# Which products of a six-group MoE kernel run in two Winograd levels: the third factor made one stage earlier, P7 of the third group split again

## The chip, the cores and the metric

The kernel runs on one core of one Trainium2 chip. Its metric is the device time of one execution in microseconds (us), lower is better; a run's time is given as the median of several executions. The profile is of one further execution, with every instruction's start and length on the core's engines: TensorE (PE, with its weight loads as PEld), VectorE (DVE), ScalarE (ACT), GpSimd (POOL) and SyncE (SP). GpSimd does no arithmetic here: it issues the software DMAs, one after the other. SyncE issues the hardware ones.

## The reference

A block of linear attention with decay, whose output is the input of a two-layer block with the activation h − tanh(h). All is in float32.

```python
# q, k, v: (B 4, H 8, S 768, D 64), blocks of 64 along S, lam one decay per head
intra = einsum('bhic,bhjc->bhij', qb, kb) * Dmask      # Dmask = lam ** (i - j), i >= j
out   = einsum('bhij,bhjd->bhid', intra, vb) + einsum('bhid,bhde->bhie', qb * lam_pow, kv_state)
kv_state = lam ** 64 * kv_state + einsum('bhsd,bhse->bhde', kb * rev_pow, vb)
# x: attention's output as (B*S 3072, H*D 512)
h = x @ w_in              # w_in  512 x 2048
g = h - tanh(h)
y = g @ w_out             # w_out 2048 x 512
```

## The kernel before, in words

**Groups and stages.** The 768 positions are cut into six groups of 128 (`g` from 0 to 5, `NG` 6), each with the 512 tokens of four batches. A group has an *up stage* (x @ w_in and the activation), a *down stage* (g @ w_out), and, in pieces laid between the products, the attention of the group after it. The loop over `g` from 1 on is one Python loop that writes the order out by hand. What is called the second group here is `g` = 1, the third `g` = 2 (the constant `GI`).

**Products.** The large matrix products are done by Winograd's form of Strassen's scheme: each matrix is cut in four, and seven products of sums of the quarters, P1 to P7, take the place of eight. `FACT` names the two sums that each product takes. In the down stage the right-hand sums come from w_out alone. They are made once, while the first group is in its down stage, and lie in DRAM in the tensor `factors`.

**Two levels.** A product can be split once more, into seven products of sums of quarters of its two factors. `twice(g, n)` says whether product n of the down stage of group g is done so. The plain form is `down`: four weight pieces of 256 KB and 16 matmuls of 256 columns, which the trace records as 32. The form in two levels is `down_twice`: seven pieces of 256 KB and 28 matmuls of 128 columns, recorded as 56. Ahead of it, `sums_twice` makes three sums of the left factor on VectorE; inside it, ScalarE copies four results out of PSUM and VectorE makes one more sum of the left factor and adds the rest up. In the kernel before, P5 and P6 are in two levels in the second group; P4, P5 and P6 in the third; all of P3 to P7 in the fourth and fifth; all but P3 in the sixth.

**Making a factor's second level.** The right-hand sums of the second level have to be made on the chip too. `MADE` gives the order of the factors: P5's, P6's, P4's, P7's, P3's, with the index t from 0 to 4. Each takes three steps. `load_quarters(t)` loads the factor's four quarters from `factors` (four DMAs of 256 KB, L770). `quarters_alone(t)` copies three quarters, that serve as they are, to the DRAM tensor `fine` (three DMAs, L775). `factors_twice(t)` makes four differences on VectorE (L782), in place in the quarters' buffers, and stores each to `fine` (four DMAs, L783). Since the differences are made in place, they must wait until `quarters_alone` has read the buffers.

In the kernel before, t = 0 and 1 are loaded ahead of the second group's up stage, and `make_factors(step)` runs their differences inside it, one difference after each of certain products: `TURNS` gives the steps, 7 to 10 and 14 to 17 of 28. A step is one product P1 to P7 of one of the four slices u of the up stage. t = 2 is loaded in the second group's down stage and its differences made in the tail of that stage; t = 3 and t = 4 likewise in the third group's, each in a buffer that a sum of the up stage (`hidden(..., "S1")`) leaves free.

**Pieces.** `piece` loads weight pieces for the down stage in the order of a list, `stream`, up to eight ahead (`RING`), into the eight buffers of the tag "wb". The quarters of t = 0 lie in the same eight buffers, those of t = 1 in buffers of output tiles.

**Other work in the second group's up stage.** `inner_weights` makes sums of w_in on VectorE (L651) for the third group and stores them (L654); `up` does the products and the activation: L576 and L581 add a PSUM bank called z to a sum, L564 subtracts the tanh; L332 and L343 belong to the next group's attention. SyncE loads q and k of later groups in small blocks.

**What sets the order.** Each engine runs its instructions in one order. A planning pass of the framework sets it: by place in the program, but an instruction that it takes to be ready sooner can be put ahead of earlier ones. `keep_in_program_order` (through `tied`) pins an instruction behind the one traced just before it on its engine. The differences in `factors_twice` are pinned on VectorE, the loads for t > 1 on GpSimd; the copies in `quarters_alone`, the stores and the piece loads are not.

Of the kernel before, what the change touches and what calls it, by code (L numbers as in the profile page):

```python
# [24 lines left out]
def kernel(  # L25
# [39 lines left out]
    NG = S // BLK  # L65
# [61 lines left out]
    def tied(yes, op):  # L127
        return tc.keep_in_program_order(op) if yes else op
# [68 lines left out]
    GI = 2  # L197
    TWICE = (3, 5, 6, 4, 7)
# [96 lines left out]
    def bank(name, tag, bufs):  # L295
        return psum.tile([128, 512], F32, name=name, tag=tag, bufs=bufs)
# [242 lines left out]
    def hidden(g, c):  # L539

        if (g, c) not in hid:
            hid[g, c] = gpool.tile([128, NU, 2, HB], F32, name=f"g{c}", tag=f"g{c}")
        return hid[g, c]
# [179 lines left out]
    RING = 8  # L723

    def twice(g, n):
        return n in TWICE and not (g == NG - 1 and n == 3) and not (g == 1 and n == 4) and not (
            g <= GI and n in (7, 3))

    def in_turn(g):

# [8 lines left out]
    def pieces_of(g):  # L739
        for n in (1, 2, 4, 5, 6, 7):  # L740
            yield from ((g, n, x) for x in (SUB if twice(g, n) else range(NU)))
        if g == NG - 1:
            yield from ((g, 3, x) for x in range(NU))
            return
        for kind, x in in_turn(g):
            if kind == "down":
                yield g, 3, x
            elif x in (3, 5, 6):
                yield g + 1, ("in", kind), x
# [7 lines left out]
    def quarter_source(t, i, j):  # L757
        return factors[XAT[FACT[MADE[t]][1]]].rearrange("p (u m) c -> p u m c", m=2)[:, :, i, ts(j, 128)]

    def load_quarters(t):  # L760

        for i in range(2):
            for j in range(2):
                if t == 0:
                    x = late["pool"].tile([128, NU, 128], F32, name="wq", tag="wb", bufs=RING)
                elif t > 1:
                    x = hidden(GI + (t > 2), "S1")[:, 2 * i + j].rearrange("p m (v c) -> p (m v) c", v=2)
                else:
                    x = opool.tile([128, NU, 128], F32, name="oq", tag="o")
                tied(t > 1, nc.gpsimd.dma_start(out=x, in_=quarter_source(t, i, j)))  # L770
                quarters[t, i, j] = x

    def quarters_alone(t):
        for x, i, j in ((1, 0, 0), (2, 1, 0), (3, 1, 1)):
            nc.gpsimd.dma_start(out=fine[TWICE.index(MADE[t]), SUB.index(x)], in_=quarters[t, i, j])  # L775

    def factors_twice(t):

        b11, b12, b21, b22 = (quarters.pop((t, i, j)) for i in range(2) for j in range(2))
        t1, t3, t4, t2 = b11, b12, b21, b22  # L780
        for x, dst, a, b in ((5, t1, b12, b11), (7, t3, b22, b12), (6, t2, b22, t1), (4, t4, b21, t2)):
            tc.keep_in_program_order(nc.vector.tensor_tensor(dst, a, b, op=AL.subtract))  # L782
            nc.gpsimd.dma_start(out=fine[TWICE.index(MADE[t]), SUB.index(x)], in_=dst)  # L783
            yield
# [21 lines left out]
    def stores_due():  # L806
        while due:
            due.pop(0)(True)

    def store(g, c, t, late_store=False):  # L810
        i, j = divmod(c - 11, 10)
        rows = out.rearrange("(b s) d -> s b d", b=B)[ts(g, BLK), 2 * i:2 * i + 2, ts(j, 256)]
        eng = nc.sync if g == NG - 1 else nc.gpsimd

        def go(held):
            tied(held, eng.dma_start(out=rows, in_=t.rearrange("q (m c) -> q m c", m=2)))

        if late_store:
            due.append(go)
        else:  # L820
            go(False)

    def otile(name):
        return opool.tile([128, 512], F32, name=name, tag="o")

    res, low = {}, {}
# [56 lines left out]
    def quarter(g, n):  # L883

        a = hidden(g, HIDAT[FACT[n][0]])
        return tuple(a[:, :, j, ts(i, 128)] for i in range(2) for j in range(2))
# [9 lines left out]
    def down_twice(g, n, zw):  # L896
        a11, a12, a21, a22 = quarter(g, n)
        s1, s2 = low.pop((g, n))
        y = bank("y2", "ya" if n in (4, 6, 3) else "yb", 1)[:, 0:128]
        zw = bank("zw", zw, 1)  # L900
        o = res[g, n] = otile(f"q{n}")
        for x, a, dst, keep in ((1, a11, y, o[:, 0:128]), (2, a12, zw[:, 0:128], None), (6, s2, y, o[:, 128:256]),
                                (5, s1, zw[:, 256:384], None), (7, a21, y, o[:, 384:512]), (3, a12, zw[:, 128:256], None),
                                (4, a22, y, o[:, 256:384])):
            wb = piece(g, n, x).rearrange("p m c -> p (m c)")
            for u in range(NU):
                tied(held["yes"], nc.tensor.matmul(  # L907
                    out=dst, lhsT=a[:, u, :], rhs=wb[:, ts(u, 128)], start=x in (1, 2) and u == 0, stop=u == NU - 1,
                    skip_group_check=True))
            if keep is not None:  # L910
                nc.scalar.activation(keep, dst, AF.Copy)  # L911
            if x == 2:
                nc.vector.tensor_tensor(a12, a12, s2, op=AL.subtract)
            if x == 5 and due:
                stores_due()
            if x != STEPS[-1]:
                yield

        o5 = o.rearrange("q (i c) -> q i c", i=2)[:, :, 128:256]
        nc.vector.tensor_tensor(o5, o5, zw[:, 256:384][:, None, :].to_broadcast([128, 2, 128]), op=AL.add)  # L920
        nc.vector.tensor_tensor(o[:, 0:256], o[:, 0:256], zw[:, 0:256], op=AL.add)
        if n == 6:

            nc.vector.tensor_tensor(o, o, res[g, 1], op=AL.add)
            for x in (4, 5):
                nc.vector.tensor_tensor(res[g, x], res[g, x], o, op=AL.add)
        elif n == 7:
            nc.vector.tensor_tensor(res[g, 4], res[g, 4], o, op=AL.add)
            store(g, 21, res[g, 4], g < NG - 1)
            nc.vector.tensor_tensor(o, o, res[g, 5], op=AL.add)  # L930
            store(g, 22, o, g < NG - 1)
        elif n == 3:
            nc.vector.tensor_tensor(o, o, res[g, 5], op=AL.add)
            store(g, 12, o)
        yield

    def every(steps):
        for _ in steps:
            pass
# [82 lines left out]
    def run(pieces):  # L1022
        for fn, *args in pieces:
            fn(*args)
# [90 lines left out]
    late["pool"] = ctx.enter_context(tc.tile_pool(name="late", bufs=1))  # L1115


    TURNS = {t + x: n for n, t in ((0, 7), (1, 14)) for x in range(4)}
    making = {}

    def make_factors(step):
        t = TURNS.get(step)
        if t is not None:
            if t not in making:
                making[t] = factors_twice(t)
            next(making[t])

    for t in range(2):
        load_quarters(t)
# [4 lines left out]
    for g in range(1, NG):  # L1134
# [69 lines left out]
            for u in (2, 3):  # L1204
                inner_weights(u, (5,))
        if g < GI:
            load_quarters(2)
        if twice(g, 7):
            sums_twice(g, 7)
        every(down_twice(g, 6, zw[0]))  # L1210
# [3 lines left out]
        p7 = down_twice(g, 7, zw[1]) if twice(g, 7) else down(g, 7)  # L1214
        next(p7)
        run(p1[4:])
        if g == GI:
            load_quarters(3)
        if g < GI:
            for u in (0, 1):  # L1220
                inner_weights(u, (6,))
# [1 line left out]
        if last:  # L1223
            down_end(g)
            continue
        if g in (1, GI):
            quarters_alone(1 + g)
        if g < GI:
            for u in (2, 3):
                inner_weights(u, (6,))  # L1230
# [5 lines left out]
        for kind, x in in_turn(g):  # L1236
            if (kind, x) == (5, 1):
                inner_tokens(g + 1, (5, 2))
                every(parts[1])
                every(p3)  # L1240
            if (kind, x) == (4, 1):
                inner_tokens(g + 1, (4, 6))
                every(parts[5])
                every(parts[2])
                if g >= GI:
                    run(early_pieces)
            if kind not in parts:
                parts[kind] = inner_steps(g + 1, kind)
            next(parts[kind])
            if kind == 1 and x in ((6, 3) if g >= GI else (3,)):  # L1250
                run(early_pieces[:1])
                early_pieces = early_pieces[1:]
            if g < GI and (kind, x) == (4, 5):
                every(factors_twice(2))
            if g == GI and (kind, x) == (1, 4):
                every(factors_twice(3))
            if g == GI and (kind, x) == (5, 7):
                load_quarters(4)
            if g == GI and (kind, x) == (4, 2):
                quarters_alone(4)  # L1260
            if g == GI and (kind, x) == (6, 7):
                every(factors_twice(4))
            if kind == 6 and x in (5, 6, 2, 7):
                seeded(g + 1, (5, 6, 2, 7).index(x), 11)
                if g < GI and x == 6:
                    run(early_pieces)
# [32 lines left out]
```

## Time and profile before

| | |
|---|---|
| median of 3 runs | 645.86 us (643.43 to 646.31) |
| the profiled execution | 642.59 us, span 640.8 us |
| TensorE busy | 632.3 us, 99% of the span, granted clock 1.00 |
| VectorE, ScalarE, GpSimd busy | 480.7, 270.9, 221.6 us |
| data moved by DMA | 139.80 MB, mean 218 GB/s |
| second group: first up to last inner product | about 139 to 276 us |
| third group, from its first down matmul to that of the fourth | 275.80 to 376.99 us |

Times within the span count from its start. "L850" is line 850 of the kernel: L850 are the plain down products, L907 those in two levels, L554 the up products of the second group, L698 and L620 those of the later groups; L796 loads a piece of a factor in two levels, L799 a plain one. Matmul ends are modelled in the trace, so distances are read from start to start. A busy TensorE is not in itself one at its peak.

### The profile page before, as it was taken

The page shows a single profiled execution, that of the slowest core. Times are in us where ns is not written, and L with a number is a line of the kernel's source. Part 1 is how long each engine was busy: PE and PEld are TensorE (multiplying, and loading weights), DVE is VectorE, ACT ScalarE, POOL GpSimd, SP SyncE. Part 2 cuts the span into 40 slices and gives each one's busy share as a digit, 9 for nine tenths or more (in the row PEclk, how much of TensorE's full clock was granted, in tenths as well). Part 3 has the DMA queues.
Part 4 walks back from the last instruction along what each step waited for, and adds up shares of the span by engine and source line. Part 5 has one row for each costly group of instructions (what it writes and reads, how often), then busy time and mean ns, then how long its engine had stood idle before and what let it go on. Part 6 is the DMA issues. An engine that isn't in the chain of part 4 may idle for free.

```text
span 640.8 us, 16604 instructions
## 1 busy us (share of the span) xinstructions
PE 632.3 (99%) x6424; PEld 580.8 (91%) x6424; DVE 480.7 (75%) x956; ACT 270.9 (42%) x626; POOL 221.6 (35%) x388
## 2 busy tenths in 40 slices
PE   8999999999999999999999999999999999999998
PEld 6788888888888999998999998999998899998997
DVE  4779697757888877579966589987658987467953
ACT  3898678403522422335431336243246332334310
POOL 0000135436623465311545730445321254421251
PEclk9999999999999999999999999999999999999999
DMA  9989899749956899876899994898873477732384
GB/s 211 230 230 246 224 280 303 268 120 287 306 134 171 244 298 316 234 159 132 246 272 279 268 318 111 212 278 266 226 194 77 136 240 239 247 107 76 100 300 144
DMA packets 166046, 139.80 MB, mean 218 GB/s; under 512 B 136720, under 2 KB 137872, under 8 KB 165968
## 3 DMA queue, kind: packets, MB, share of 16 engines
q0 software_dynamic: 31648, 104.62, 50.4%
q1 hardware_dynamic: 134176, 34.12, 26.2%
q8 instruction: 51, 0.84, 0.5%
q14 instruction: 27, 0.22, 0.1%
q10 hardware_dynamic: 144, 0.00, 0.0%
HBM read 111.94 MB, written 26.74 MB: 216 GB/s over the span
## 4 chain that ended last, share of the span: by engine, by line
PE 79%; issue 10%; POOL 4%; DMA 3%; DVE 2%; SPq 1%; ACT 1%; POOLq 0%
PE plain L850 12%; PE y L698 8%; PE y L907 8%; PE acc L995 7%; PE y L554 7%; PE zw L907 6%; PE z L698 4%; PE y L620 3%; PE zs L620 3%; PE z L554 3%; PE h L966 3%; POOL wb L796 2%; PE w L698 2%; PE w L554 2%; PE op L498 2%
## 5 line engine op out<-in xcount | busy, mean ns | idle before, releaser
L796 POOL DMA_DIRECT2D wb<-fine x133 | 71.6, 539 | 156.8 <-PE plain L850 107.9
L850 PE MATMUL plain<-wb,g 128*128 128x256 f32 x416 | 96.0, 381 | 0.0
L850 PEld LDWEIGHTS plain<-wb,g 128*128 128x128 f32 x416 | 77.5, 190 | 10.4
L911 ACT ACTIVATE q<-y 128x128 f32<-128x128 f32 x76 | 21.1, 277 | 85.2 <-PE y L907 84.1
L799 POOL DMA_DIRECT2D wb<-factors x64 | 34.5, 539 | 62.4 <-PE z L698 40.4
L907 PE MATMUL y<-wb,g 128*128 128x128 f32 x336 | 44.8, 278 | 0.0
L793 POOL DMA_DIRECT2D wb<-fine_in x60 | 32.5, 543 | 27.8 <-PE z L698 10.8
L601 ACT ACTIVATE th<-g 128x512 f32<-128x512 f32 x48 | 29.5, 627 | 29.4 <-DVE g L626 29.3
L907 PEld LDWEIGHTS y<-wb,g 128*128 128x128 f32 x336 | 40.7, 192 | 0.7
L689 ACT ACTIVATE g<-y 128x512 f32<-128x512 f32 x24 | 14.3, 597 | 63.1 <-PE y L698 63.1
L218 POOL DMA_DIRECT2D raw<-in_moe_w_out_dram x12 | 7.1, 592 | 87.8 <-ACT r L290 84.1
L401 ACT ACTIVATE k_nat<-k_nat,mask 128x64 f32<-128x64 f32 (+1 forms) x128 | 35.0, 336 | 0.6 <-DMA k_nat<-in_k_dram 0.6
L995 PE MATMUL acc<-wt,g 128*128 128x256 f32 x144 | 32.7, 380 | 0.0
L602 DVE TENSOR_TENSOR g<-g,th 128x512 f32<-128x512 f32 x48 | 32.0, 683 | 0.4
L698 PE MATMUL z<-tt,wb 128*128 128x128 f32 x256 | 31.9, 275 | 0.0
L966 PE MATMUL h<-xt,w 128*128 128x256 f32 x128 | 29.9, 383 | 1.2 <-DVE w L293 1.2
L995 PEld LDWEIGHTS acc<-wt,g 128*128 128x128 f32 x144 | 27.0, 190 | 4.1 <-DVE g L1003 0.4
L620 PE MATMUL y<-xt,w 128*128 128x256 f32 x128 | 30.3, 379 | 0.0
L620 PE MATMUL zs<-xt,ws 128*128 128x256 f32 x128 | 30.2, 379 | 0.0
L698 PEld LDWEIGHTS z<-tt,wb 128*128 128x128 f32 x256 | 30.2, 192 | 0.0
L907 PE MATMUL zw<-wb,g 128*128 128x128 f32 x224 | 30.1, 277 | 0.0
L966 PEld LDWEIGHTS h<-xt,w 128*128 128x128 f32 x128 | 23.6, 190 | 4.6 <-ACT xt L459 0.8
(237 smaller groups left out, 1541.6 us busy)
## 6 DMA issues: line engine op xcount, KB each, us to landing
wb<-fine POOLq DMA_DIRECT2D x133, 256.0 KB, 4.1
wb<-factors POOLq DMA_DIRECT2D x64, 256.0 KB, 4.4
wb<-fine_in POOLq DMA_DIRECT2D x60, 256.0 KB, 4.6
v_nat<-in_v_dram SPq DMA_DIRECT2D x24, 256.0 KB, 5.0
raw<-in_moe_w_out_dram POOLq DMA_DIRECT2D x12, 512.0 KB, 5.6
fine<-gS POOLq DMA_DIRECT2D x21, 256.0 KB, 6.0
k_nat<-in_k_dram SPq DMA_DIRECT2D x20, 256.0 KB, 5.3
raw<-in_moe_w_in_dram SPq DMA_DIRECT2D x8, 512.0 KB, 5.1
```

The source lines that it names most:

```text
L401: tc.keep_in_program_order(nc.scalar.activation(k_h, k_h, AF.Copy, scale=mask[0:rows, h % 2, h // 2, HALF - 1:HALF]))
L554: tied(held["yes"], nc.tensor.matmul(out=t[:, m, :], lhsT=wt[:, kt, ts(m, 128)], rhs=x[:, kt, :], start=first and m == 0 and kt == 0, stop ...
L602: nc.vector.tensor_tensor(dst(c), src, th, op=AL.subtract)
L620: nc.tensor.matmul(out=t[:, m, :], lhsT=wt[:, kt, ts(m, 128)], rhs=x[:, kt, :], start=False, stop=kt == 1, skip_group_check=True)
L698: nc.tensor.matmul(out=dst[:, ts(u, 128)], lhsT=a, rhs=b, start=(x in (1, 5) or x == 2 and not filled) and u == 0, stop=True, skip_group_c ...
L793: nc.gpsimd.dma_start(out=t.rearrange("p m c -> p (m c)"), in_=fine_in[INNER.index(n_[1]), (5, 6, 3).index(x_)].rearrange("p u c -> p (u c)"))
L796: nc.gpsimd.dma_start(out=t.rearrange("p m c -> p (m c)"), in_=fine[TWICE.index(n_), SUB.index(x_)].rearrange("p u c -> p (u c)"))
L799: nc.gpsimd.dma_start(out=t, in_=factors[XAT[FACT[n_][1]]][:, 2 * x_:2 * x_ + 2, :])
L850: tied(held["yes"], nc.tensor.matmul(out=t[:, m, :], lhsT=a[:, u, kt, ts(m, 128)], rhs=wb[:, kt, :], start=first and u == 0 and m == 0 and ...
L907: tied(held["yes"], nc.tensor.matmul(out=dst, lhsT=a[:, u, :], rhs=wb[:, ts(u, 128)], start=x in (1, 2) and u == 0, stop=u == NU - 1, skip ...
L966: tied(u == 0 or held["yes"], nc.tensor.matmul(out=hm[c][:, m, :], lhsT=w1[u][:, i, a, ts(m, 128)], rhs=xt[0, t][:, i, :], start=m == 0 an ...
L995: tied(held["yes"], nc.tensor.matmul(out=acc[n][:, r, :], lhsT=a[:, ts(r, 128)], rhs=b, start=kt == 0 and r == 0, stop=kt == KH - 1, skip_ ...
```

## The change

P7 of the third group is done in two levels. For that, the second level of P7's factor (t = 3) has to be there by the third group, so it is made where P4's (t = 2) was, in the second group's down stage, in the same buffer; and t = 2 moves to the second group's up stage: its quarters are loaded at step 11 into four of the eight piece buffers, its three copies follow in the program after step 17, and its differences come after steps 18 to 21. The work for t = 3 goes from the third group's tail; t = 4 stays there. Whether P7's two output stores are put off is now asked by `twice(g, 3)` instead of `g < NG - 1`: for the third group they are issued at once, as its plain P7's were.

```diff
     def twice(g, n):
-        return n in TWICE and not (g == NG - 1 and n == 3) and not (g == 1 and n == 4) and not (
-            g <= GI and n in (7, 3))
+        return n in TWICE and not (g == NG - 1 and n == 3) and not (g < GI and n in (4, 7)) and not (
+            g <= GI and n == 3)
...
     def load_quarters(t):
-                if t == 0:
+                if t in (0, 2):
                     x = late["pool"].tile([128, NU, 128], F32, name="wq", tag="wb", bufs=RING)
                 elif t > 1:
-                    x = hidden(GI + (t > 2), "S1")[:, 2 * i + j].rearrange("p m (v c) -> p (m v) c", v=2)
+                    x = hidden(GI + (t > 3), "S1")[:, 2 * i + j].rearrange("p m (v c) -> p (m v) c", v=2)
...
         elif n == 7:
-            store(g, 21, res[g, 4], g < NG - 1)
+            store(g, 21, res[g, 4], twice(g, 3))
-            store(g, 22, o, g < NG - 1)
+            store(g, 22, o, twice(g, 3))
...
-    TURNS = {t + x: n for n, t in ((0, 7), (1, 14)) for x in range(4)}
+    TURNS = {t + x: n for n, t in ((0, 7), (1, 14), (2, 18)) for x in range(4)}
     def make_factors(step):
         t = TURNS.get(step)
         if t is not None:
             if t not in making:
                 making[t] = factors_twice(t)
             next(making[t])
+        if step == 11:
+            load_quarters(2)
+        if step == 17:
+            quarters_alone(2)
...
         if g < GI:
-            load_quarters(2)
+            load_quarters(3)
...
         next(p7)
         run(p1[4:])
-        if g == GI:
-            load_quarters(3)
...
-        if g in (1, GI):
-            quarters_alone(1 + g)
+        if g < GI:
+            quarters_alone(3)
...
             if g < GI and (kind, x) == (4, 5):
-                every(factors_twice(2))
-            if g == GI and (kind, x) == (1, 4):
                 every(factors_twice(3))
```

## The prediction

> **What bounds the kernel now.** I read the page's busy rows first, then the busy time by stretch, then TensorE's timeline at P7, then VectorE's and GpSimd's timelines in the second group's up stage, where the change adds its work.
>
> ```profile
> PE 632.3 (99%) x6424; PEld 580.8 (91%) x6424; DVE 480.7 (75%) x956; ACT 270.9 (42%) x626; POOL 221.6 (35%) x388
> ...
> 100.00:600.00 500.00, 500.00 (x5064) 463.41 (x5064) 380.99 (x760) 190.87 (x472) 195.96 (x339) 1.00 0.75 216
> ```
>
> The second row has the stretch's length and then the busy us of PE, PEld, DVE, ACT and POOL, the granted clock, the DMA share and GB/s. From 100 to 600 us PE is busy 500.00 of 500.00 at clock 1.00. All that the change touches lies inside. So no wait is there to be removed: the end moves by the matmul time that goes, and by any wait that is newly made.
>
> ```profile
> 330.46 1.99 PE L850 MATMUL plain<-wb,g 128*128 128x256 f32 x8
> 332.39 1.16 PE L498 MATMUL op<-ss,v_nat 64*64 64x64 f32 x64
> 333.48 7.17 PE L850 MATMUL plain<-wb,g 128*128 128x256 f32 x32
> 340.49 1.05 PE L698 MATMUL y<-xt,w 128*128 128x128 f32 x8
> ...
> 431.65 1.16 PE L907 MATMUL y<-wb,g 128*128 128x128 f32 x8
> 432.81 1.16 PE L498 MATMUL op<-ss,v_nat 64*64 64x64 f32 x64
> 433.90 1.16 PE L907 MATMUL zw<-wb,g 128*128 128x128 f32 x8
> 434.90 1.06 PE L907 MATMUL y<-wb,s 128*128 128x128 f32 x8
> ```
>
> Columns are start, length, engine, line, operation. Above is P7 of the third group, plain, with eight matmuls, an attention piece, then its other 24 run on into eight of P3. Below is P7 of the fourth group, in two levels, around the same attention piece: this is what the third group gets.
>
> ```profile
> 176.00:184.00 8.00, 8.00 (x38) 7.04 (x38) 6.59 (x18) 3.13 (x8) 1.00 (x2) 1.00 0.38 87
> ...
> 177.54 0.69 DVE L581 TENSOR_TENSOR g<-g,z 128x512 f32<-128x512 f32 x1 [0.35 <-PE z L554]
> ...
> 193.77 0.69 DVE L564 TENSOR_TENSOR g<-y,th 128x512 f32<-128x512 f32 x1 [2.70 <-ACT th L563]
> ...
> 168.50 0.54 POOL L799 DMA_DIRECT2D wb<-factors  x1 [0.95 <-DMA fine<-wq]
> ...
> 182.82 0.76 POOL L654 DMA_DIRECT2D fine_in<-ws  x1 [7.43 <-DVE ws L651]
> ...
> 180.79 1.89 PE L554 MATMUL z<-tt,ws 128*128 128x256 f32 x8
> ```
>
> Here the new work must fit: DMA is only 0.38 busy from 176 to 184, GpSimd's queue stands idle 7.43 us, VectorE has gaps, and TensorE starts a new sum in bank z at 180.79, which the VectorE read at 177.54 has to have left.
>
> **The change part by part.** *P7 of the third group.* Plain: 332.39 − 330.46 = 1.93 for the first eight; from 333.48 to 340.49 is 7.01 for 32, of which eight of the same kind take 1.73 elsewhere (342.27 to 344.00, the next product's), so 5.28 for 24; sum 7.21. Two levels, seven steps of eight: 432.81 − 431.65 = 1.16, 434.90 − 433.90 = 1.00, four steps from there to 438.47 in 3.57, the last 0.89; sum 6.62. That is 0.59 less. A second reading: from the third group's first down matmul to the fourth's is 376.99 − 275.80 = 101.19, the next such distance is 476.94 − 376.99 = 99.95, and the later group has two more products in two levels: 1.24, or 0.62 each. Ends 0.59 and 0.62; I take 0.6, on the path.
>
> *What P7 adds beside it.* VectorE gets three sums over 512 columns (L891 to L893, spaced 0.60), one more (L913) and two half-wide adds (L920, L921, 0.42): some 3.2 us. ScalarE gets four copies (L911, 0.28): 1.1 us. GpSimd issues three more piece loads (L796, 0.54): 1.6 us. From the same group go four subtractions (L782, spaced 0.60: 2.4 us) and eleven DMAs of 256 KB. The two output stores stay direct and of the same size. The fourth group runs all of this already, with two-level P3's sums besides, in a stretch where PE is busy 25.00 of 25.00 us (420 to 445). The tightest place there is L913, done at 428.08, for a matmul at 428.68: 0.6 us margin. Cost 0; without that cover each us of VectorE past the margin costs one. Bounds: 0, and 0.6, if the margin is missed by as much again.
>
> *The P7 factor at the third factor's old place.* Same count of loads, copies, subtractions and stores, in the same buffer and place. Cost 0; below nothing is excluded, since PE does not wait there.
>
> *The third factor in the second group's up stage: VectorE.* Four L782, 2.4 us. They are pinned behind the additions traced just before them, so the first stands behind the L564 that ends at 176.33. From there to 193.77 VectorE idles 0.17 + 0.35 + 0.76 + 2.70 = 3.98, so it has caught up by 193.77. Before that the nearest date is bank z: the read at 177.54 ends at 178.23 and PE needs it by 180.79, 2.56 margin. Up to three subtractions go ahead of the read: 1.8 less the gaps 0.17 and 0.35 leaves it 1.3 late, 1.2 to spare. Cost 0; past 1.2 us each us is PE's.
>
> *The same: queues.* On GpSimd four loads (L770, 0.75), three copies (L775, 0.54) and four stores (L783, 0.56) are 6.9 us; the idle 7.43 us before 182.82 and those before 170.41 hold them. Behind them wait the inner stores (L654), needed only in the next stage, and loads of weight pieces. The new loads take four of the eight piece buffers, so that four P2 pieces, now loaded from 165.32 to 168.50, come after the new stores have landed. The last store would go out by 183.2 and land by some 188 (L654 issued there land after 2.5 to 3.7, L783 at 170 to 174 after 3.0 to 3.5), the pieces by 192 or 193 (4.2 after, as at 186.44). P2 begins at 196.72: 4 us margin, cost 0. SyncE's queue is not passed by any of it, but its blocks share the DMA engines: eleven transfers, 2.9 MB, are some 9.6 us at 300 GB/s, and from 176 to 200 the shares 0.38, 0.67 and 0.39 leave 12.5 us idle. The last block of the group landed at 201.49 for a transpose at 213.77.
>
> *The same: the new wait.* The subtractions write over the buffers that the three copies read, so they wait for load plus copy in series. The trace has no such chain this close to its subtraction; bounds are from its other rounds, first load issued to third copy landed: 145.05 to 158.41 (13.4), 227.40 to 244.00 (16.6), 330.27 to 343.24 (13.0). The new loads can start at 163.7, behind the store they are pinned to, or at 165.3, if they wait for the buffers as the pieces do now. So the third copy lands between 176.7 and 181.9. The third subtraction would run at 177.9; then 0.60 for it and 0.69 for the read of z: PE loses nothing if the copy lands by 179.5, and at 181.9 it loses 2.4. I take 0, by 13.4, the round of this very stage (177.1 to 178.7). Ends: 0 and 2.4.
> The Trainium skill, page "DMA: Bandwidth & Descriptors", section "Anatomy of one DMA", gives about 2.0 us plus the bytes over 436 GB/s; by that estimate a 256 KB transfer is 2.6, two in series 5.2, the copies would be home before 172 and this bound would vanish. The trace does not agree: these loads land 5.0 to 7.7 us after issue.
>
> Sum: −0.6. The profiled execution took 642.59 (span 640.8 and 1.79 around it), so 642.0 for it; it stands 3.27 under the median of the three runs. On the median 645.86 the forecast is **645.2**.
>
> **The rivals.** *B, the copies come late* (slower). The place is the third subtraction, ahead of the read of bank z; it decides from a landing at 179.5 on. If the three copies are queued in their written place, behind the store at 174.64, they go out at 175.4, 175.9 and 176.5 and land 6 us later, as the first three L775 of this stage (5.9 to 6.8), at 182.5; z is read until 183.8 and PE, due at 180.79, loses 3.0; a landing at 183.3 would lose 3.8. With the 0.6 saved that is 645.86 + 2.4 = 648.3, 649.1 at that far end. For it: DMA is 0.95 busy from 160 to 176. Against: copies are not pinned, and the four piece loads leave that stretch.
>
> *C, P2's pieces late.* If the pieces queue behind the loads that P1 releases (the last at 191.61, landed 195.61), the four go out by 194 and land from 196.2 on; perhaps 0.5 us: 645.7.
>
> *D, narrow matmuls are bound by their weight loads.* A load takes 192 ns (L907) as wide ones do (190, L850). At a load each, 56 would be 10.8 instead of 7.2: +3.6, 649.4. Against it: eight narrow steps take 0.89, or 112 ns each, so loads overlap.
> The Trainium skill, page "TensorE: Matmul & The Clock Gate", section "Back-to-back issue gap", has 81 ns per matmul at 128 columns and 131 at 512; a line between them, an estimate, gives 98 at 256, so that 56 narrow for 32 wide would be 1.45 times the time, 3.2 us more here. The trace differs: 112 against 216 ns, 0.52.
>
> *E, a larger gain.* Eleven DMAs leave the third group's tail, where DMA is 0.95 busy. A gain past 3.2 us needs PE idle time there, and there is none; what is left is scatter, as in the profiled run: 642.0.
>
> **How the numbers follow.** Chances: forecast 0.71, B 0.18, C 0.06, D 0.01, E 0.04. A measurement tells about 0.5% (3.2 us) from no change; the three runs themselves differ by 2.9. Faster by more: E and a little of the forecast's scatter, 0.05. Slower by more, above 649.1: D, the far end of B and an order of instructions that I cannot see, 0.12. Within: 0.83. The range goes down by the runs' scatter below the forecast, to 643.0, and up to B's main case, 648.3; the likeliest alone is 643.8 to 646.0.
>
> **What would show it.** Right: P7 of the third group is 56 matmuls of 128 columns in 6.6 us; the distance between the third and fourth groups' first down matmuls falls to 100.6; PE stays busy 500.00 of 500.00. Wrong: a gap of PE before z at about 181, with VectorE's L782 waiting for fine<-wq (B), or before P2 waiting for wb (C).

## The result, and the profile after

The changed kernel takes 645.92 us, the kernel before 643.63 us (medians of 22 runs each, taken in turns): a ratio of 1.0033, with a 95% interval from 1.0017 to 1.005. By the ratio that is 2.1 us slower, where 0.6 us faster was forecast; the two medians differ by 2.29. It lies inside the half per cent and inside the range, on the other side of no change. That 645.92 stands only 0.7 us above the forecast of 645.2 is chance: the forecast was counted from 645.86, the median of three executions, and 22 put the kernel before at 643.63. The profiled execution took 647.28 us with a span of 645.5, and so shows more of the loss than the median does.

TensorE's row of the page and its stretch from 100 to 600 us, in the changed kernel (columns as before):

```profile
PE 632.7 (98%) x6448; PEld 580.9 (90%) x6448; DVE 483.9 (75%) x962; ACT 272.2 (42%) x630; POOL 223.3 (35%) x391
...
100.00:600.00 500.00, 495.44 (x5064) 458.95 (x5063) 378.91 (x756) 188.62 (x470) 197.11 (x341) 1.00 0.76 216
```

In the kernel before it was 500.00 of 500.00. Now 4.56 us are idle, at the same clock of 1.00. A little of it, 0.71 us at 113, lies in the first group, ahead of anything that was changed. The rest must be found by place. The timeline of TensorE around P7 of the third group in the changed kernel comes first, since that is the part that was to bring the gain:

```profile
336.63 1.16 PE L907 MATMUL y<-wb,g 128*128 128x128 f32 x8
337.79 1.16 PE L498 MATMUL op<-ss,v_nat 64*64 64x64 f32 x64
338.88 1.16 PE L907 MATMUL zw<-wb,g 128*128 128x128 f32 x8
339.87 1.06 PE L907 MATMUL y<-wb,s 128*128 128x128 f32 x8
...
344.34 1.89 PE L850 MATMUL plain<-wb,g 128*128 128x256 f32 x8
```

P7 takes 337.79 − 336.63 = 1.16 and 344.34 − 338.88 = 5.46, together 6.62 us, the number that was worked out, against 7.21 plain. The gain is there. The loss lies more than 40 us earlier, in the up stage of the same group. First TensorE, then ScalarE, both in the changed kernel:

```profile
287.28 1.89 PE L850 MATMUL plain<-wb,g 128*128 128x256 f32 x8
290.60 1.99 PE L620 MATMUL y<-xt,w 128*128 128x256 f32 x8 [1.43 <-ACT y L610]
...
294.47 1.89 PE L850 MATMUL plain<-wb,g 128*128 128x256 f32 x8
298.09 1.99 PE L620 MATMUL y<-xt,w 128*128 128x256 f32 x8 [1.73 <-ACT y L610]
```

```profile
281.78 1.23 ACT L601 ACTIVATE th<-g 128x512 f32<-128x512 f32 x2 [2.73 <-DVE g L626]
289.00 1.06 ACT L401 ACTIVATE k_nat<-k_nat,mask 128x64 f32<-128x64 f32 x4 [5.99 <-DMA k_nat<-in_k_dram]
289.97 0.58 ACT L610 ACTIVATE y<-g 128x512 f32<-128x512 f32 x1
```

In brackets stand the idle time ahead of an instruction and what ended it. TensorE waits for a seed: the value that ScalarE writes into a PSUM bank (L610) before a product is added to it. The seed stands on ScalarE behind L401, which scales the fourth group's k for the attention's state, and ScalarE is idle for 5.99 us ahead of L401 until that k has landed. The same place in the kernel before:

```profile
282.48 1.06 ACT L401 ACTIVATE k_nat<-k_nat,mask 128x64 f32<-128x64 f32 x4 [0.58 <-DMA k_nat<-in_k_dram]
283.45 0.58 ACT L610 ACTIVATE y<-g 128x512 f32<-128x512 f32 x1
...
286.17 1.89 PE L850 MATMUL plain<-wb,g 128*128 128x256 f32 x8
...
293.07 1.89 PE L620 MATMUL y<-xt,w 128*128 128x256 f32 x8
```

Here too L401 waited, for 0.58 us, and TensorE did not. This k was just in time before the change, and the row that said so was there to be read. From the first of the two TensorE rows to the second is 6.90 us; in the changed kernel it is 298.09 − 287.28 = 10.81, so 3.9 us are lost here from start to start, more than the 3.16 us that the two waits show. Why k is later now is seen on SyncE's queue. First the kernel before, then the changed one; a row is the issue of so many loads one after the other, with the pauses between them. The last two rows of each are for the loads of L153 from 172 to 200 us: a wait of SyncE (us in all, times, longest), and the time from issue to landing:

```profile
173.78 8.22 SPq L153 DMA_DIRECT2D k_blk<-in_k_dram  x16
182.04 8.94 SPq L153 DMA_DIRECT2D q_blk<-in_q_dram  x16
191.10 8.87 SPq L153 DMA_DIRECT2D k_blk<-in_k_dram  x16
200.08 0.39 SPq L140 DMA_DIRECT2D k_nat<-in_k_dram  x1
...
277.84 0.39 SPq L140 DMA_DIRECT2D k_nat<-in_k_dram  x1
...
SPq L153 <- DMA k_blk<-in_k_dram: 0.4, 1, 0.4
...
DMA to landing us min/median/max: 1.6/2.8/4.3
```

```profile
172.19 10.53 SPq L153 DMA_DIRECT2D k_blk<-in_k_dram  x16
183.67 9.44 SPq L153 DMA_DIRECT2D q_blk<-in_q_dram  x16
193.22 10.95 SPq L153 DMA_DIRECT2D k_blk<-in_k_dram  x16
204.28 0.41 SPq L140 DMA_DIRECT2D k_nat<-in_k_dram  x1
...
285.58 0.39 SPq L140 DMA_DIRECT2D k_nat<-in_k_dram  x1
...
SPq L153 <- DMA k_blk<-in_k_dram: 3.6, 7, 0.9
...
DMA to landing us min/median/max: 3.0/5.1/7.5
```

The queue goes on from one group's loads to the next group's: in these rows there is always a next load to issue. Sixteen block loads that took 8.2 to 8.9 us take 9.4 to 10.9 while the moved transfers run. The issue of one is no slower, 0.43 to 0.44 us in the median in both kernels; what grows is the wait between two. In the trace the loads of this queue take eight semaphores in turn, and each waits for the one before it on its semaphore, that is, for the landing of the load eight places back. So the load at 179.21 was issued 0.02 us after the load of 173.35 had landed, at 179.19. Unhindered, issues follow each other every 0.47 to 0.48 us (182.04, 182.51, 182.99 in the kernel before), so that eight take some 3.8 us, an estimate from these rows: a load that takes longer to land holds the queue. The median landing rose from 2.8 to 5.1 us, and the pauses of over 0.1 us between 172 and 200 from 1.1 to 6.4 us in all.

By 204.28 the queue is 4.2 us behind, of which 0.8 is a later start of the whole execution (P1 of the second group begins at 185.09 in place of 184.25). By the fourth group's k it is 7.7 us behind, and k lands at 288.98 in place of 282.46. Why it loses 3.5 us more on that way, with the moved transfers done, is not shown; in another execution of the changed kernel (below) the same loads were 4.1 us behind at 204.22 and 3.2 at k. The DMA share of the changed kernel in the stretch that the prediction showed:

```profile
176.00:184.00 8.00, 8.00 (x38) 7.03 (x37) 7.30 (x14) 3.94 (x10) 5.45 (x9) 1.00 0.97 308
```

It is 0.97 where it was 0.38. The transfers did go into idle bandwidth, and the quick landings of SyncE's loads had hung on that idleness.

### The profile page after: what moved, and what is told of

Read it like the earlier page. It is cut to its first block, busy times and chain, and to the rows that moved or that the text cites. A ratio compares the mean times of both kernels' runs of the same rounds, so it can differ in the third digit from the quotient of the medians.

```text
span 645.5 us, 16675 instructions
## 1 busy us (share of the span) xinstructions
PE 632.7 (98%) x6448; PEld 580.9 (90%) x6448; DVE 483.9 (75%) x962; ACT 272.2 (42%) x630; POOL 223.3 (35%) x391
## 4 chain that ended last, share of the span: by engine, by line
PE 71%; DMA 11%; DVE 7%; ACT 5%; SPq 4%; issue 2%; DVEq 0%; ACTq 0%
PE y L907 10%; PE plain L850 9%; PE y L698 8%; PE zw L907 8%; PE y L554 5%; PE acc L995 4%; PE z L698 4%; DMA k_blk<-in_k_dram 4%; DMA q_blk<-in_q_dram 3%; PE y L620 3%; PE zs L620 3%; PE z L554 3%; SPq L153 3%; PE w L698 2%; PE op L498 1%
## 5 line engine op out<-in xcount | busy, mean ns | idle before, releaser
L796 POOL DMA_DIRECT2D wb<-fine x140 | 75.4, 539 | 165.8 <-PE plain L850 111.4
L850 PE MATMUL plain<-wb,g 128*128 128x256 f32 x384 | 88.7, 381 | 0.0
L850 PEld LDWEIGHTS plain<-wb,g 128*128 128x128 f32 x384 | 71.5, 190 | 9.5
L799 POOL DMA_DIRECT2D wb<-factors x60 | 32.3, 540 | 59.4 <-PE z L698 41.9
L907 PE MATMUL y<-wb,g 128*128 128x128 f32 x360 | 48.1, 278 | 0.0
L907 PEld LDWEIGHTS y<-wb,g 128*128 128x128 f32 x360 | 43.6, 192 | 0.7
L401 ACT ACTIVATE k_nat<-k_nat,mask 128x64 f32<-128x64 f32 (+1 forms) x128 | 35.0, 336 | 6.0 <-DMA k_nat<-in_k_dram 6.0
L907 PE MATMUL zw<-wb,g 128*128 128x128 f32 x240 | 32.4, 278 | 0.1
L620 PEld LDWEIGHTS y<-xt,w 128*128 128x128 f32 x128 | 24.0, 190 | 7.4 <-ACT y L610 4.0
```

What stands on the lines that cost most here:

```text
L401: tc.keep_in_program_order(nc.scalar.activation(k_h, k_h, AF.Copy, scale=mask[0:rows, h % 2, h // 2, HALF - 1:HALF]))
L620: nc.tensor.matmul(out=t[:, m, :], lhsT=wt[:, kt, ts(m, 128)], rhs=x[:, kt, :], start=False, stop=kt == 1, skip_group_check=True)
L796: nc.gpsimd.dma_start(out=t.rearrange("p m c -> p (m c)"), in_=fine[TWICE.index(n_), SUB.index(x_)].rearrange("p u c -> p (u c)"))
L799: nc.gpsimd.dma_start(out=t, in_=factors[XAT[FACT[n_][1]]][:, 2 * x_:2 * x_ + 2, :])
L850: tied(held["yes"], nc.tensor.matmul(out=t[:, m, :], lhsT=a[:, u, kt, ts(m, 128)], rhs=wb[:, kt, :], start=first and u == 0 and m == 0 and ...
L907: tied(held["yes"], nc.tensor.matmul(out=dst, lhsT=a[:, u, :], rhs=wb[:, ts(u, 128)], start=x in (1, 2) and u == 0, stop=u == NU - 1, skip ...
```

## The experiments

The theories were these. *Q, the queue*: the eleven transfers of the third factor hold up SyncE's block loads, the fourth group's k comes late, and ScalarE's order hands the lateness to TensorE. *S, the split*: P7 in two levels costs more than it gives. *V, VectorE*: the four subtractions hold things up. Ratios are to the kernel before, timed in turns on the same chip, with 95% intervals.

### The split alone

```diff
# the kernel before, with the new twice() and store conditions
-  in_=fine[TWICE.index(n_), SUB.index(x_)] ...
+  in_=fine[TWICE.index(4 if (g_, n_) == (GI, 7) else n_), SUB.index(x_)] ...
```

> The kernel before with P7 of the third group in two levels, and nothing else moved: every factor is made where it was. The seven pieces of that P7 are read from P4's second level, which is there in time, so the third group's P7 is a product with the wrong factor. Theory Q (queue: the transfers moved into the second group's up stage hold up SyncE's block loads, the fourth group's k arrives late, and ScalarE's queue behind it holds TensorE): no wait in the third group's up stage, k lands there as in the kernel before (about 282.5 us), P7 takes 6.6 us in place of 7.2, time 0.6 us under before (ratio 0.999, between 0.9975 and 1.0005). Theory S (split: two levels in the third group cost more than they give, on VectorE or by pieces that come late): slower than before by about 2 us, ratio 1.003.

Measured: 1.0059 (1.0047 to 1.0071). Slower, and so a miss for Q's number; it is what S expected, pieces that come late. k was not late (L401 ran at 282.52 without a wait), the third group's up stage had no gap, and P7 took 6.6 us. TensorE's only gap between 100 and 600 lies behind P7, in P3. The second and third rows are GpSimd's queue ahead of it, the last is the stretch behind it, with the clock third from the end:

```profile
344.91 2.98 PE L850 MATMUL plain<-wb,g 128*128 128x256 f32 x8 [2.35 <-DMA wb<-factors]
...
339.69 0.55 POOL L775 DMA_DIRECT2D fine<-gS  x1 [1.78 <-DMA gS<-factors]
340.23 0.54 POOL L799 DMA_DIRECT2D wb<-factors  x1
...
346.00:349.00 3.00, 3.00 (x12) 2.64 (x11) 0.00 (x0) 0.00 (x0) 1.98 (x4) 0.50 0.98 324
```

In this kernel the P7 factor (t = 3) is still made in the third group's tail. The piece of P3 stands on GpSimd's queue behind two copies that wait for their quarters, and goes out at 340.23, where it went at 337.08 in the kernel before; it landed at 344.87. The gap of 2.35 us cost more than its length: behind it the clock granted to TensorE was 0.50 from 346 to 349, and from start to start 338.88 to 349.29 is 10.41 us, where the same products took 6.13 before (338.76 to 344.89): 4.3 us lost. The three more pieces of P7 and t = 3's transfers did not go together in that tail. So this run does not price the split by itself; it shows what the split meets if t = 3 stays in the tail.

### The move alone

```diff
# the changed kernel
-            g <= GI and n == 3)
+            g <= GI and n in (7, 3))
```

> The changed kernel with the third group's P7 plain again; both factors are still made at their new places. Theory Q: the wait in the third group's up stage is as in the changed kernel, the fourth group's first k lands some 6 us later than before, and the 0.6 us of the split are missing as well: 2.1 + 0.6 = 2.7 us slower than before, ratio 1.004 (1.002 to 1.006). Theory S: as before, ratio 1.000.

Measured: 1.0049 (1.0029 to 1.0068). L401 waits 5.05 us for k (landed 287.18), and TensorE waits 0.49 and 1.73 us for seeds. The loss is there without the split: 3.1 us (1.9 to 4.4) by the ratio. S falls as the cause of the result.

### The same transfers without the subtractions

```diff
# the changed kernel, in factors_twice
-            tc.keep_in_program_order(nc.vector.tensor_tensor(dst, a, b, op=AL.subtract))
+            if t != 2:
+                tc.keep_in_program_order(nc.vector.tensor_tensor(dst, a, b, op=AL.subtract))
```

> The changed kernel without the four subtractions of the third factor on VectorE; the four stores write the quarters as loaded, so P4's factor is wrong from the third group on. All eleven transfers are made. Theory Q: the wait stays, k lands as late as in the changed kernel (some 6 us after before's), ratio 1.003 (1.001 to 1.005). Theory V: the wait goes, ratio 0.999.

Measured: 1.0089 (1.0067 to 1.0112). L401 waits 5.22 us for a k that lands at 288.08. V falls as the cause of the late k. That this kernel is slower still than the changed one is not explained by k alone: without the subtractions the stores go out in another order, and TensorE also waits 0.55 us at the start of P1. How far its runs' spread (646.39 to 650.97) comes from that was not followed further.

### The split with the third factor's transfers left out

```diff
# the changed kernel
-        if step == 11:
-            load_quarters(2)
-        if step == 17:
-            quarters_alone(2)
-    TURNS = ... ((0, 7), (1, 14), (2, 18)) ...
+    TURNS = ... ((0, 7), (1, 14)) ...
-  in_=fine[TWICE.index(n_), SUB.index(x_)] ...
+  in_=fine[TWICE.index(7 if n_ == 4 else n_), SUB.index(x_)] ...
```

> The changed kernel with the third factor's eleven transfers and four subtractions left out; nothing takes their place in the second group's up stage. P4's second level is never made; the P4 pieces are read from P7's instead, so P4 is a product with the wrong factor from the third group on. The last runs showed the wait with P7 plain, and also without the subtractions, and another wait where P7 was split with the fifth-factor work still in the third group's tail; what is open is what the split gives when no transfer is in its way. Theory Q (the eleven transfers hold up SyncE's queue, k comes late): no wait in the third group's up stage, k lands at about 282.5 us, P3's pieces are in time, ratio 0.999 (0.9975 to 1.0005). Theory S (the split has its own price): 1.001 or more, with a gap of TensorE in the third group's down stage.

Measured: 0.9984 (0.9971 to 0.9998). With the eleven transfers gone, k lands at 280.46, and TensorE's stretch from 100 to 600 is full but for 0.17 us:

```profile
100.00:600.00 500.00, 499.83 (x5092) 464.45 (x5091) 383.08 (x763) 192.60 (x476) 192.02 (x332) 1.00 0.73 212
```

This kernel is 0.1 to 1.9 us faster than the kernel before by the interval; the 0.59 us read from the timeline lies in it. It makes one factor fewer than the kernel before, so the split's own price is read more surely from P7's place in the timeline: from the third group's first down matmul to the fourth's is 100.60 us here (276.18 to 376.78), as the prediction had it, against 101.19 before and 105.65 in the changed kernel.

### SyncE's queue made late by other means

```diff
# the kernel before; load_again issues twelve of the sixteen loads of the fourth group's first q block again
                 load_blocks(g, b, "qk")
+                if g == GI + 1 and b == 0:
+                    load_again(g, b)
```

> The kernel before with twelve of the fourth group's first 16 KB block loads done twice on SyncE's queue: some 6.5 us more on that queue, 0.2 MB more data, nothing on GpSimd's queue or VectorE. Theory Q: k of the fourth group lands some 6 us later, at about 289, ScalarE is held there and TensorE waits in the third group's up stage as in the changed kernel, ratio 1.004 (1.002 to 1.007). If it is DMA volume or GpSimd's queue that counts, and not SyncE's lateness: 1.000.

Measured: 1.0054 (1.0035 to 1.0073). GpSimd and VectorE run what they ran before, and twelve small loads bring back the picture: k lands at 287.34, ScalarE waits for it, and TensorE for two seeds. ScalarE and TensorE in this kernel (its line numbers are ten higher):

```profile
287.37 1.06 ACT L411 ACTIVATE k_nat<-k_nat,mask 128x64 f32<-128x64 f32 x4 [5.53 <-DMA k_nat<-in_k_dram]
...
288.97 1.99 PE L630 MATMUL y<-xt,w 128*128 128x256 f32 x8 [0.97 <-ACT y L620]
296.45 1.99 PE L630 MATMUL y<-xt,w 128*128 128x256 f32 x8 [1.73 <-ACT y L620]
```

Lateness of that one queue is enough; no further transfer of 256 KB is needed for it.

### k ahead in SyncE's order

```diff
# the changed kernel, in load(); x not in first: from the fourth group on
             for b in range(B - 1):
+                if b == 2:
+                    for x in (0, 1):
+                        if x not in first:
+                            load_natural(g, x, nat)
                 load_blocks(g, b, "qk")
             load_blocks(g, 3, "q")
-            for b in (0, 1):
-                if b not in first:
-                    load_natural(g, b, nat)
```

> The changed kernel, with SyncE's order changed from the fourth group on: k and v of batches 0 and 1 are loaded ahead of the blocks of batch 2 in place of behind those of batches 2 and 3; the same loads otherwise. Theory Q: k of the fourth group's batches 0 and 1 lands before 270 us, some 15 us ahead of ScalarE's scaling of it, no wait of TensorE in the third group's up stage, and the time is 0.6 us under before: ratio 0.999 (0.997 to 1.001). Theory S, and theory V (VectorE: it is the four subtractions in the up stage that hold things up): still 2 us slower, ratio 1.003.

Measured: 0.9985 (0.9976 to 0.9993). The same loads and the same eleven transfers, another order on the queue, and the changed kernel, called k_first below, is faster than the kernel before. k landed at 267.18. The one gap left, 0.96 us at 221.6, is the second group's product of k and v for the state, whose loads (batch 3 of the third group, landed 212.73 and 213.78) still stand at the end of the late queue.

### The kernel before with that order

The edit is the one above, on the kernel before.

> The kernel before with SyncE's order changed as in k_first. Theory Q: there was no wait for k to be removed, so no difference: ratio 1.000 (0.999 to 1.001). If the order of loads is itself worth 0.1% or more, k_first's gain was not the split's: ratio 0.9985.

Measured: 1.0007 (0.9994 to 1.0021). The order by itself is worth nothing that can be measured, so what k_first gains is the split's. In k_first, too, the distance between the two groups' first down matmuls is 100.60 us.

### ScalarE's order in place of SyncE's

```diff
# the changed kernel, third group's up stage
-                some(kd, 2)
+                some(kd, 0 if u == 0 and g == GI else 2)
```

> The changed kernel; only ScalarE's scaling of the fourth group's k starts one slice later in the third group's up stage, so that fewer seeds and tanh stand behind it; loads and transfers as in the changed kernel. Theory Q: k still lands at about 289 us, but the seeds and tanh of slices 0 and 1 no longer wait for it; TensorE's waits of 1.4 and 1.7 us there go, ratio 0.999 to 1.001. If something other than ScalarE's order ties TensorE to that k: still 1.003.

Measured: 1.0000 (0.9987 to 1.0012). k lands at 286.93, as late as in the other disturbed kernels, and no seed waits for it: the two gaps are gone. 0.65 us are left at 298.7, where the state's product with that k waits. So the lateness became a loss because the scaling stood ahead of the seeds on ScalarE's queue.

### The changed kernel once more, and batch 3 moved too

The first is the changed kernel as it is; the second is k_first with this:

```diff
-            load_blocks(g, 3, "k")
+            load_blocks(g, 3, "k", (lambda: load_natural(g, 3, nat)) if first else None)  # after 8 of the 16 loads
```

> The changed kernel as it is, on the same chip as the runs beside it. Theory Q: the fourth group's first k lands some 6 us later than before, ScalarE waits 5 to 6 us for it and TensorE some 3 us in the third group's up stage; less the 0.6 us of the split 2 to 3 us slower: ratio 1.003 to 1.005.

> k_first, with k and v of the third group's batch 3 loaded in the middle of that group's last 16 block loads in place of after them. In k_first TensorE still waited 0.96 us at 221.6 for the state product that reads them (landed 212.73 and 213.78). Theory Q: they land some 4 us earlier, that wait goes, and the time is between k_first's and 0.6 to 1.0 us under it: ratio to before 0.998 (0.997 to 0.9995). If the last blocks then come late for VectorE's transpose at 214, nothing is gained: 0.9985.

Measured: 1.0043 (1.0021 to 1.0066) and 0.9985 (0.9976 to 0.9993). The repeat agrees with the result. Its profiled execution happened to be its fastest, 642.38 us, and so shows the other end of the same mechanism. ScalarE and TensorE's stretch there, and then the stretch in the second kernel:

```profile
284.07 1.06 ACT L401 ACTIVATE k_nat<-k_nat,mask 128x64 f32<-128x64 f32 x4 [1.80 <-DMA k_nat<-in_k_dram]
...
100.00:600.00 500.00, 499.22 (x5088) 463.77 (x5087) 384.23 (x766) 192.16 (x475) 198.28 (x342) 1.00 0.76 217
```

```profile
100.00:600.00 500.00, 500.00 (x5093) 464.36 (x5092) 385.33 (x768) 192.39 (x476) 198.84 (x343) 1.00 0.75 217
```

With k at 284.04, L401 waits 1.80 us and no seed comes late; TensorE has 0.78 us idle, none of it in that stage. Most of it is a wait for VectorE's L913 at 313, in P4, which costs 0.9 us from start to start; the move alone and the kernel with the queue made late have it too, k_first has not. The changed kernel's runs reach here from 642.38 to 650.10, those of k_first only from 641.39 to 642.76. With batch 3 moved as well, k and v of that batch land at 203.27 and 205.55, and TensorE is busy 500.00 of 500.00 again. Against k_first that is no measurable step; both are 0.15% under the kernel before.

## Why the prediction was wrong

The forecast was 0.6 us faster; 2.1 us slower was measured. The gain was priced rightly; a cost that had been put at nothing was not nothing.

- *P7 in two levels.* Right to the hundredth in the timeline (6.62 us), and the work beside it was hidden as said: the distance to the next group fell to the 100.6 us that were forecast in the runs where no k was late and the third group has no gap. The rivals D and E fell with it. The Trainium skill's page "TensorE: Matmul & The Clock Gate", section "Back-to-back issue gap", would have had the narrow form lose, by the prediction's estimate from its two figures. The trace does not agree: 6.62 us against 7.21.
- *VectorE in the second group's up stage.* Right. The subtractions ran at 177.09, 178.29, 179.49 and 182.87, and VectorE had caught up by 194.61, with 1.59 us idle ahead of it (2.70 before).
- *The new wait, and rival B.* Right to take 0. The copies landed at 174.17, 176.33 and 177.04, the read of z ran at 178.89, and TensorE began its next sum in z at 181.63 without a gap. B's sign was right and its place was wrong, so it does not count for the mechanism.
- *GpSimd's queue, and rival C.* Right: P2's pieces came later, behind a wait of 3.96 us, and P2 began without a gap.
- *SyncE's queue.* This is the step that failed: "SyncE's queue is not passed by any of it, but its blocks share the DMA engines", priced at nothing because 12.5 us of idle DMA time covered 9.6 us of transfers, and because the last block of that group had 12 us in hand. Both numbers hold, and neither was the one that mattered. Idle DMA time says whether the transfers fit, not how long a small load takes to land among them, and it is the landing of the load eight places back that lets this queue go on (median landing 5.1 us in place of 2.8). The queue has little slack in which to catch up, so what slows it in one group can still be there at the next group's loads. The price was to be read at every later user of that queue, up to the first that has no margin: L401 at 282.48, which already waited 0.58 us in the kernel before. That the late k is the cause is shown by the same loss with the queue made late alone (1.0054), and by its absence with k ahead in the queue (0.9985), with the scaling moved back on ScalarE (1.0000), and without the transfers and subtractions (0.9984). Without the subtractions alone k still lands at 288.08.
- *The size.* 2.1 + 0.6 = 2.7 us is an estimate of the late k's mean price; the move alone measured 3.1. It varies from execution to execution with the landing of k: no seed is late at 284.04 and 0.9 us go at 313, while at 288.98 two seeds are late and 5.0 us go between 287 and 319, from start to start.

None of the rivals had this case, neither within the half per cent nor in the 0.12 beyond it; they looked for waits in the stage that was changed, and the wait was in the next group's up stage.

## What to carry to other kernels

A queue that always has a next load to issue has little slack of its own: when anything is moved into its bandwidth, ask how long its loads will take to land, and follow it forward, past the stage, to the first user that is already waiting a little. A row with a short wait on an engine that nobody calls a bound can be where the next microsecond shows. And when such a user stands in front of critical work on an in-order engine, the order of loads, or of the user, is the cheaper thing to change: here the loads' order turned a loss of 0.3 to 0.4% into a gain of 0.15%, and the user's brought it to no change.

## What the runs showed of the hardware that was not expected

The landing of small loads slowed, not their issue. From 172 to 200 us the 16 KB block loads on SyncE's queue landed 2.8 us after issue in the median in the kernel before and 5.1 in the changed one; from 176 to 184 the DMA share was 0.38 and 0.97. The issue of one took 0.43 to 0.44 us in both. With eight loads under way at most, the later landings stretched sixteen of them from 8.2 to 10.5 us. In the kernel before, such a row reached 15.9 us later in the span.

A wait of TensorE can cost more than its length. In the split alone, after 2.35 us without work, the granted clock was 0.50 from 346 to 349. After the waits of 1.43 and 1.73 us in the changed kernel it stayed at 1.00.

The time of the changed kernel, run once more, spread over 7.7 us (642.38 to 650.10), that of k_first, in another set of runs, over 1.4. It is not shown that a wide spread tells of such a wait: the kernel before had one run at 647.73 among 23 that otherwise ended at 643.84, and the kernel whose queue was made late, with the wait in its trace, spread over 0.9 only (646.25 to 647.17). The three longest of those runs of the changed kernel (646.80 to 650.10) had a mean granted clock of 0.997; no trace of them is kept, so how much of their time is the clock's stays open.
